# Turned sums in both chains, three PSUM rounds for the backward products, loads on another queue and split stores in a memory-transformer kernel

## The chip, the cores and the metric

The kernel runs on one core of one Trainium2 chip. The metric is device time in microseconds (us) of one execution. Ratios to "before" are each from the fast runs of the same rounds and with a 95% interval; a ratio is not quite the quotient of the medians quoted beside it. Chips differ by some tenths of a per cent (the kernel before had medians from 3278 to 3294 us), so ratios, not microseconds, are compared across batches. One per cent is 33 us.

## The reference, cut to what matters

The function is a transformer block whose attention runs segment by segment with a memory of 8 rows handed from each segment to the next. The kernel computes the output and all gradients.

```python
for s in range(n_seg):                       # 2048 rows, 64 segments of 32 rows
    h = concat([mem, xs])                    # 8 memory rows + 32 rows
    q, k, v = h@Wq, h@Wk, h@Wv               # 32 heads of 128
    p = softmax(mask(q k^T * scale))
    o = (p v) @ Wo                           # back to 512 columns
    mem = o[:, :8]; outs.append(o[:, 8:])
y = x + attention(layernorm(x)) + squared_relu_mlp(layernorm(x))
# returned: y and the gradients of x, mem0, Wq, Wk, Wv, Wo, w1, b1, w2, b2
```

Memory makes 64 forward steps and 64 backward steps strictly serial. These are the *forward chain* and the *backward chain* below. Work on the 8 memory rows that can wait is done per block of four steps; its instructions are called *leftover* here, and their names begin with `L.`

## The kernel before

The four engines read one ordered list of short operation names. Each engine executes its own operations in the order of that list and waits on semaphores where data is missing. A name's last digit is the half of the heads (0 or 1).

A backward step goes as follows. The gradient of the step's output, GT, is projected (`o0mm o1mm`), copied to SBUF as gON (`o0ev o1ev`), turned (`o0fl o1fl`) and copied as gOT (`o0te o1te`). Products of short vectors give the gradient of v (`vp`). Scores (`s0 s1`) and four VectorE instructions (`d1 d2 d3 d4`) give the softmax gradient gS; the last of them, `d4`, writes gS. `tu` turns gS. Products with gS give the gradients of k and q (`kp`, `qp`). Each product round lands in PSUM and is copied out ("evicted") to gv, gk, gq, with `e` for the 32 rows of the step and `l` for the 8 rows of memory. Six *gathers* (`vg kg qg`, 16 matmuls each) sum everything into one PSUM bank, R. R holds four row groups of 32 which must be added up and turned to give the next step's GT.

Before, the adding was a copy, a matmul against a selection matrix, a copy, and a transpose:

```python
def sm():                                    # 4 matmuls: adds the row groups
    ps["n"] = alloc("ps_sum")
    for c in range(DC):
        nc.tensor.matmul(ps["n"][SEG * c:SEG * c + SEG, 0:P], lhsT=sel[:], rhs=R4()[:, c * P:(c + 1) * P],
                         start=True, stop=True, tile_position=(0, SEG * c), skip_group_check=True)
def sF():
    ps["F"] = F()
    ENGS[pre + "sF"](ps["F"][:], ps["n"][:, 0:P])
def sT():
    nc.tensor.transpose(ps["n"][:, P:2 * P], ps["F"][:], identF[:])
    ...
```

Products used six rounds a step (v0 v1 k0 q0 k1 q1), all in the same pair of PSUM tiles, with 20 evictions. The list for one of the four steps of a block, the loads and the stores:

```python
B_ORDER = (
    "o0mm o0ev xt- L.xt- o1mm o0fl vp0 L.lq o1ev o0te o1fl s0 vea0 veb0 o1te ldq- ldn- L.qo ldk- vtr vg0 "
    "vlb0 d10 vla0 vp1 d20 d30 s1 L.G0 veb1 L.H0 d11 vlb1 vla1 d40 vea1 d21 tu0 kp0 kea0 klb0 keb0 d31 vg1 "
    "d41 kla0 qp0 qea0 qeb0 ldp kg0 tu1 kp1 kea1 klb1 L.sx- keb1 kla1 qg0 qp1 ldn qea1 qeb1 L.ra0 kg1 qg1 "
    "ra L.G1 sm vc sF L.H1 sT HT",
    ...                                      # three more steps, cut
# ---- cut ----
o["ldq"] = lambda: dma(tile_of("qN", [P, GW])[:], rows[:, GW:2 * GW])      # dma = nc.sync.dma_start
...
def vc():                                    # assembles vT for the next step's scores
    vT = tile_of("vT", [P, KH, HG, L])
    nc.gpsimd.tensor_copy(vT[:, :, :, 0:SEG], C["vl"][:])
    nc.gpsimd.tensor_copy(vT[:, :, :, SEG:L], B_["vTL"][:, :, :, lc])
```

## Time and profile before

The time before is 3290.86 us (two runs, 3289.17 to 3292.55). Of the profiled execution these are the head of the page, with the busy time of engines (and their share of the span and instruction count), the TensorE clock in 40 slices (9 is full), and the DMA queues (packets, MB, share of the 16 DMA engines).

```profile
span 3266.8 us, 115469 instructions
PE 2704.2 (83%) x51673; PEld 1338.9 (41%) x51768; DVE 1220.4 (37%) x3526; ACT 1017.1 (31%) x2492; POOL 193.7 (6%) x345
PEclk9999899999999999966799999999999988999999
q1 hardware_dynamic: 890418, 625.81, 77.0%
q8 instruction: 406, 6.65, 0.8%
```

PE is the line that everything hangs on. Its idle time is the loss. So the view to read is PE's waits, taken for the backward chain alone (from its first projection to its last, 1602 to 2608 us). Columns: the waiting instruction, what it waited for, then total us, number of waits, longest.

```profile
PE b_pp L563 <- issue: 45.8, 34, 4.7
PE ps_gR L478 <- issue: 18.5, 15, 2.8
PE ps_proj L437 <- DVE GT L424: 17.9, 63, 0.3
PE ps_sum L497 <- ACT F L421: 17.3, 47, 0.4
PE ps_sum L489 <- ACT R L421: 13.3, 18, 0.8
PE b_pp L563 <- DMA b_qN<-S_A: 12.3, 11, 2.7
PE ps_sc L458 <- DVE gOT L424: 3.5, 16, 0.2
PE b_pp L563 <- DVE gS L522: 1.8, 4, 0.7
```

The largest item is "issue", time in which PE waited for nothing the profile shows. All lines of that kind sum to 73.8 us. The trace shows next to these gaps a 16 KB instruction page that starts late: the 2.94 us gap at 1860.01 us has its page start 0.47 us into it. I call them *page stalls*.

| stage | us |
|---|---|
| forward chain, first to last projection | 890.6 |
| backward chain, first to last projection | 1005.4 |
| from there to the end (weight gradients) | 659 |

### The profile page before, as it was taken

What the parts mean: (1) busy time and instruction counts of PE and PEld (TensorE: products, weight loads), DVE (VectorE), ACT (ScalarE), POOL (GpSimd) and SP (SyncE); (2) the same over time, 40 slices, a digit from 0 to 9 for tenths busy, and PEclk for the clock granted to TensorE, in tenths of its full rate; (3) what the DMA queues carried; (4) which work ended last, traced back from release to release, by engine and by line L of the source; (5) the groups of instructions that cost most, each with busy time, mean ns of one, the idle gap of its engine ahead of it and who ended that gap; (6) DMA issues with size and microseconds to landing.
All of it is one profiled execution on the core that took longest, in us unless ns stands there. A gap on an engine that the chain in (4) does not pass through costs nothing.

```text
span 3266.8 us, 115469 instructions
## 1 busy us (share of the span) xinstructions
PE 2704.2 (83%) x51673; PEld 1338.9 (41%) x51768; DVE 1220.4 (37%) x3526; ACT 1017.1 (31%) x2492; POOL 193.7 (6%) x345
## 2 busy tenths in 40 slices
PE   8898778888888888834688888888888866999998
PEld 4453334444444444412344344344344423444444
DVE  4440035555655555523344344444444400010001
ACT  3331124444444444412333333333333401111111
POOL 0000000000000000000000010010000000000000
PEclk9999899999999999966799999999999988999999
DMA  9958894676667676689668666666776699999993
GB/s 254 283 145 312 293 291 114 165 179 162 185 164 184 161 184 161 171 235 256 185 164 210 166 164 181 189 164 172 190 183 172 173 260 199 205 186 224 187 187 91
DMA packets 890915, 633.20 MB, mean 194 GB/s; under 512 B 659745, under 2 KB 748466, under 8 KB 881074
## 3 DMA queue, kind: packets, MB, share of 16 engines
q1 hardware_dynamic: 890418, 625.81, 77.0%
q8 instruction: 406, 6.65, 0.8%
q14 instruction: 91, 0.75, 0.1%
HBM read 227.16 MB, written 250.10 MB: 146 GB/s over the span
## 4 chain that ended last, share of the span: by engine, by line
PE 57%; DMA 13%; SPq 13%; DVE 7%; issue 5%; ACT 5%; ACTq 0%; POOLq 0%; POOL 0%; DVEq 0%
PE ps_gR L478 11%; PE ps_proj L437 11%; PE ps_gw L1364 8%; SPq L1289 6%; PE b_pp L563 3%; PE ps_R L478 3%; DMA S_GOL<-l_gON 3%; PE ps_tr L167 2%; ACT R L421 2%; PE ps_sum L489 2%; PE ps_L L406 2%; DMA out_dram<-wt 2%; PE ps_w L366 2%; PE ps_w L386 1%; PE ps_RL L1071 1%
## 5 line engine op out<-in xcount | busy, mean ns | idle before, releaser
L1364 PE MATMUL ps_gw<-gn,HNc 128*128 128x512 bf16 x1881 | 416.5, 380 | 8.3 <-ACT wt L1339 6.3
L437 PE MATMUL ps_proj<-Wqkv,X 128*32 128x512 bf16 x6144 | 361.9, 385 | 18.2 <-DVE X L424 17.9
L1364 PEld LDWEIGHTS <-HNc 128*128 128x128 bf16 x1920 | 188.2, 98 | 231.9 <-issue 9.5
L421 ACT CAST f_N<-ps_proj 128x512 bf16<-128x512 f32 x320 | 185.4, 583 | 258.0 <-PE ps_proj L437 243.7
L1339 ACT CAST wt<-ps_gw 128x512 bf16<-128x512 f32 x126 | 69.5, 591 | 541.8 <-DMA out_dram<-wt 353.1
L437 PEld LDWEIGHTS <-X 128*32 128x32 bf16 x6144 | 156.9, 98 | 174.7 <-DVE X L424 29.9
L1322 DVE TENSOR_TENSOR gx<-ps_rows,gb 128x512 f32<-128x512 f32 x16 | 11.1, 692 | 427.5 <-PE ps_rows L1320 396.8
L1364 PE MATMUL ps_gw<-GOc,gn 128*128 128x512 bf16 x627 | 142.2, 387 | 19.2 <-DMA gn<-S_ON 18.3
L478 PE MATMUL ps_gR<-WT,b_gq 128*32 128x512 bf16 x2048 | 145.2, 401 | 7.8 <-issue 7.5
L478 PE MATMUL ps_gR<-WT,b_gk 128*32 128x512 bf16 x2048 | 145.8, 404 | 5.8 <-issue 5.7
L478 PE MATMUL ps_gR<-WT,b_gv 128*32 128x512 bf16 x2048 | 142.5, 393 | 7.6 <-issue 7.5
L437 PE MATMUL ps_proj<-WoT,GT 128*32 128x512 bf16 x2048 | 125.6, 388 | 22.5 <-DVE GT L424 17.9
L478 PE MATMUL ps_R<-Wo,OT 128*32 128x512 bf16 x2048 | 127.1, 390 | 0.0
L1145 POOL COPY b_vT<-b_vl 128x1024 bf16<-128x1024 bf16 x64 | 66.7, 1042 | 905.9 <-PE ps_sc L458 521.4
L421 ACT CAST gON<-ps_proj 128x512 bf16<-128x512 f32 x128 | 75.0, 586 | 118.9 <-PE ps_proj L437 115.2
L489 PE MATMUL ps_sum<-R,sel 128*32 128x128 f32 x1152 | 61.2, 285 | 58.4 <-ACT R L421 53.0
L1364 PEld LDWEIGHTS <-gn 128*128 128x128 bf16 x640 | 63.6, 100 | 96.4 <-DMA gn<-S_ON 18.6
L406 PE MATMUL ps_L<-Wqkv,XL 128*128 128x512 bf16 x376 | 84.8, 385 | 18.2 <-DMA XL<-S_XL 16.8
L421 ACT CAST b_gq<-b_pp 128x256 bf16<-128x256 f32 x128 | 47.7, 373 | 161.4 <-PE b_pp L563 153.3
L421 ACT CAST b_gk<-b_pp 128x256 bf16<-128x256 f32 x128 | 47.8, 373 | 150.7 <-PE b_pp L563 115.5
L424 DVE CAST b_gq<-b_pp 128x256 bf16<-128x256 f32 x128 | 54.4, 425 | 107.0 <-PE b_pp L563 102.8
L437 PEld LDWEIGHTS <-GT 128*32 128x32 bf16 x2048 | 49.5, 98 | 78.4 <-DVE GT L424 30.0
(214 smaller groups left out, 4427.9 us busy)
## 6 DMA issues: line engine op xcount, KB each, us to landing
S_A<-f_N SPq DMA_DIRECT2D x64, 512.0 KB
out_dram<-wt SPq DMA_DIRECT2D x154, 128.0 KB
S_A<-f_N SPq DMA_DIRECT2D x64, 256.0 KB
S_ON<-OC SPq DMA_DIRECT2D x64, 256.0 KB
b_qN<-S_A SPq DMA_DIRECT2D x64, 256.0 KB
b_kN<-S_A SPq DMA_DIRECT2D x64, 256.0 KB
S_GB<-b_gv SPq DMA_DIRECT2D x16, 1024.0 KB
S_GB<-b_gk SPq DMA_DIRECT2D x16, 1024.0 KB
```

What stands on the lines that cost most here:

```text
L167: nc.tensor.transpose(ps_ap, in_ap, ident[base:base + k, base:base + k])
L366: nc.tensor.matmul(ps[:], lhsT=aN[:, rc, fc * P:(fc + 1) * P], rhs=gN[:, rc, :], start=(rc == 0), stop=(rc == TC - 1))
L406: nc.tensor.matmul(ps[:], lhsT=XL[:, dc, q * P:(q + 1) * P], rhs=Wqkv[:, dc, c0:c0 + 512], start=(dc == 0), stop=(dc == DC - 1))
L421: nc.scalar.copy(out, in_)
L437: nc.tensor.matmul(ps[32 * g:32 * g + 32, :], lhsT=hT[:, dc, :], rhs=W[:, dc, c:c + 4 * P], start=(dc == 0), stop=(dc == DC - 1), tile_pos ...
L478: nc.tensor.matmul(R[32 * g:32 * g + 32, :], lhsT=XT(k, g), rhs=W[:, g * KH + k, :], start=(first and k == 4 * h), stop=(last and k == 4 * ...
L489: nc.tensor.matmul(ps["n"][SEG * c:SEG * c + SEG, 0:P], lhsT=sel[:], rhs=R4()[:, c * P:(c + 1) * P], start=True, stop=True, tile_position= ...
L563: nc.tensor.matmul(o, lhsT=N_[32 * g:32 * g + m, kk * P:(kk + 1) * P], rhs=X(kk)[32 * g:32 * g + m], start=(i == 0), stop=(i == len(jobs) ...
L1145: nc.gpsimd.tensor_copy(vT[:, :, :, 0:SEG], C["vl"][:])
L1289: nc.sync.dma_start_transpose(t_[:, b, :].rearrange("p (k e) -> p k e", k=KH), blocks(b)[:, g].rearrange("p k r -> p (k r)"))
L1339: nc.any.tensor_copy(wt[:], ps[:])
L1364: nc.tensor.matmul(ps[:], lhsT=l(rc), rhs=r(rc), start=(n == 0), stop=(n == RC_ALL - 1))
```

## The change

Intent: shorten the serial tail of each step (three PSUM crossings become two), save instructions and PSUM rounds in the backward products, take loads off the SyncE queue where they stand behind stores, and halve the 1 MB stores. The core of the diff, with cuts:

```diff
-    def sum_ops(o, alloc, R4, F, st, pre=""):        # sm sF sT: select matmul, copy, transpose
+    def turn_ops(o, alloc, R4, st):                  # ta tb: four float32 transposes of R
+            nc.tensor.transpose(st["T"][:, c * P:(c + 1) * P], R4()[:, c * P:(c + 1) * P], identF[:])
+    def over_groups(out, T, rows):                   # then one reduction over the row groups
+            nc.vector.tensor_reduce(out, T[:].rearrange("p (c g r) -> p c r g", c=DC, g=HG)[:, :, rows], ...)
...
-            def ra():                                # one copy of R
+            def ra(h):                               # two half copies: ra on ScalarE, rb on VectorE
...
-                    outer(pp("k", p), p, ...)        # six rounds: v0 v1 k0 q0 k1 q1
+                    outer(pp(p), p, ...)             # three: v (both halves), k0+q0, k1+q1
+                    outer(pp(p), p, ..., 4 * KW)     # q beside k, at a column offset
...
-            o["ldq"] = lambda: dma(tile_of("qN", ...
+            o["ldq"] = lambda: pdma(tile_of("qN", ...  # pdma = nc.gpsimd.dma_start; 320 loads in all
...
-                o[n + "o"] = lambda n=n, t=t: dma(S_GB[b, t], B_["g" + n][:]...)
+                for x in range(2): ...               # two half stores of 512 KB
...
 B_ORDER = (
+        "L.xt- o0mm vtr xt- o1mm L.lq o0ev o0fl o1ev o0te vp0 vp1 o1fl L.sx- vea veb o1te s0 s1 L.G0 vc d10 d20 "
+        "vla vlb d30 d40 vg0 d11 tu0 d21 kp0 qp0 kea0 keb0 kla0 klb0 qea0 qeb0 d31 d41 ldp vg1 L.H0 tu1 kp1 ldq "
+        "qp1 ldn ldk kg0 L.ra0 kea1 keb1 qea1 qeb1 kla1 klb1 qg0 kg1 qg1 L.G1 ra rb L.H1 ta tb HT",
```

ScalarE has `o1te vea vla vlb` among others, VectorE the `d` instructions, `veb keb0 klb0 qeb0`.

## The prediction

> **What bounds the kernel.** The page gives PE 2704 of 3267 us busy (83%); DVE 37%, ACT 31%. By stretches of the timeline: forward chain 486-1390 us (64 steps, 14.1 us each), backward chain 1600-2640 (64 steps, 16.2 us each); the change touches only these. In both, PE is the line and its idle time is the loss (waits of PE). Forward: 78 us around the sums of a step (on R 39, on F 21, on X 18), 38 on OT and ET. Backward (1640-2630): 76 us "issue" in 56 stalls of up to 4.7 us, mostly after the 1 MB block stores, so I read them as late instruction pages behind long packets; 47 us around the sums; 12 us on qN, 2 on kLs.
>
> **The sums.** Chain of waits: from the last gather matmul to the next projection 2.18 us (ACT copy 0.59, select matmul 0.47, copy 0.28, transpose 0.34, cast 0.20, rest hops). After: two 128x256 copies (ACT 0.37, DVE 0.42), four float32 transposes (four took 0.66), one reduction of 128 elements (the strided 128x32<-128x128 reduction took 0.37). Both copies read one PSUM bank. The trace has ACT's XT copy waiting for DVE's GT cast of the same bank (15 times, 9.7 us), and the Trainium skill, "PSUM — Partial Sum Buffer", on bank collisions, says two engines must not touch one bank at once, so I expect rb behind ra: 0.37+0.42+0.44+0.37 plus hops, 1.85 us. Gain 0.3 us a step, 20 us per chain; were the copies parallel, 0.7 us. XT becomes a strided reduction on DVE (0.6 instead of 0.25 us), off the path; the leftover's four reductions (1.2 us on DVE, before 0.27 on ACT) hold the first forward step of each block some 0.5 us: 8 us back. Forward: -12 us.
>
> **Backward rounds.** Rounds did not stall PE before (b_pp waits on no eviction). Four ACT/DVE instructions a step go, which were not on the path. The new order makes PE wait: walking one step with traced durations, o1te stands behind the 0.59 us eviction vea on ACT, so the second score group waits about 0.6 us; d31 and d41 stand behind keb0, klb0, qeb0 on DVE, so kp1 waits about 0.7 us with only part filled by leftover gathers. Clean step about 15.0 instead of 14.4 us, tail gain included: +40 us.
>
> **Queues.** Loads on GpSimd no longer queue behind waits on SP (SP's waits: 203 us for gS, 143 for b_pp): the 14 us on qN and kLs go. The Trainium skill, "DMA: Bandwidth & Descriptors", on issuing engines, says all queues share 16 DMA engines, so bytes cost the same; this trace has no GpSimd DMA. Half-size stores should shorten the instruction stalls; I take off 45 of 76 us, the least certain term.
>
> **Sum.** 3291 - 12 + 40 - 14 - 45 = about 3260 us. Range 3200 to 3325. Chances: faster by over 2% 0.26, within 2% 0.66, slower 0.08.
>
> **Right or wrong.** Right if: rb starts when ra ends; PE idle on X/GT near 0.4 us a step; new PE waits on gOT (ACT) and on gS near 0.6 us a step; no waits on qN; "issue" waits of PE under 40 us; forward chain shorter by 10-20 us, backward by 0-40. Wrong if: the copies run in parallel (50 us faster); stalls of issue vanish (30 faster) or stay or grow with a third ring (45 slower); GpSimd's descriptor work delays b_vT or the loads; the new waits are filled.

## The result, and the profile after

The time after is 3337.03 us (two runs, 3333.58 to 3340.49). The ratio is 1.0144, with a 95% interval of 1.0119 to 1.0168: slower, by less than 2%, and 77 us from the 3260 predicted, outside its range. The same head of the page for the kernel after:

```profile
span 3331.8 us, 113823 instructions
PE 2735.0 (82%) x50873; PEld 1372.5 (41%) x50968; DVE 1373.4 (41%) x3701; ACT 921.3 (28%) x2124; POOL 370.6 (11%) x665
PEclk9999889999999999766898998999899987999999
q1 hardware_dynamic: 876658, 556.06, 69.0%
q0 software_dynamic: 22528, 69.75, 7.1%
```

PE has 800 fewer instructions and yet 31 us more busy time. The clock row shows one reason: more 8s in the second half. GpSimd's busy time includes its DMA issues. PE's waits in the backward chain after (1586 to 2663 us):

```profile
PE ps_sc L456 <- ACT gOT L419: 41.7, 61, 0.7
PE b_pp L563 <- DVE gS L522: 39.8, 53, 0.9
PE b_pp L563 <- issue: 36.6, 22, 3.4
PE ps_proj L435 <- DVE GT L498: 24.2, 63, 0.4
PE ps_gR L476 <- issue: 19.0, 18, 4.1
PE ps_sum L485 <- ACT R L419: 10.1, 18, 1.0
PE b_pp L563 <- DMA b_qN<-S_A: 5.7, 1, 5.7
PE b_pp L563 <- DMA b_P<-S_A: 5.3, 2, 4.9
```

Two waits that were 5.3 us are now 81.5, one of each nearly every step. Page stalls went from 73.8 to 65.4 us. The forward chain went from 890.6 to 868.2 us, the backward chain from 1005.4 to 1076.4, the rest to the end from 659 to 669.

How the two waits arise can be read from the timeline of one step after (start us, duration us, engine, line, operation; in brackets the idle time before it and what ended it):

```profile
2142.99 0.59 ACT L419 CAST gv<-b_pp 128x512 bf16<-128x512 f32 x1 [0.52 <-PE b_pp L563]
2143.15 0.28 PE L456 MATMUL ps_sc<-b_vT,gOT 128*32 128x40 bf16 x16
2143.48 0.59 ACT L419 COPY gOT<-ps_tr 128x512 bf16<-128x512 bf16 x1
...
2144.12 0.28 PE L456 MATMUL ps_sc<-b_vT,gOT 128*32 128x40 bf16 x16 [0.69 <-ACT gOT L419]
...
2144.56 1.04 POOL L1144 COPY b_vT<-b_vl 128x1024 bf16<-128x1024 bf16 x1 [10.74 <-PE ps_sc L456]
2144.71 1.07 DVE L522 SCALAR_TENSOR_TENSOR gS<-ds_t,b_P 128x160 bf16<-128x160 f32 x1
```

The gOT copy (`o1te`) stands behind the eviction of gv (`vea`) on ScalarE, so the second scores wait 0.69 us. The instruction that writes gS took 1.07 us while GpSimd copied vT; its usual time is 0.33 us. The Trainium skill, "SBUF — State Buffer", section "Who interferes with whom", says that a VectorE instruction with two SBUF inputs contends with a GpSimd instruction that reads SBUF. This trace agrees: 57 of 126 gS instructions took over 500 ns, against 9 before, where the vT copy mostly fell elsewhere, and each of the 57 ended 0.17 to 0.19 us after the vT copy that it had begun in. Yet this slow instruction, in all 57 cases that of the first half, is not what PE mostly waits for. Of the 39.8 us of waits on gS 37.0 stand before the second k product, which needs the second half's `d41`, and `d41` stands behind three VectorE evictions (`keb0 klb0 qeb0`) in the list.

The half copies of R did not overlap. The group of the VectorE half (count, busy us and mean ns, then idle time before it and what ended it):

```profile
L422 DVE COPY R<-ps_gR 128x256 f32<-128x256 f32 x64 | 27.2, 425 | 245.1 <-ACT R L419 245.1
```

All its wait is for the ScalarE half. The Trainium skill, "PSUM — Partial Sum Buffer", section "PSUM bank collisions raise a hardware error", gives as the simple form of its rule that accesses to one bank are to be guarded by semaphores; the program orders the two copies, as this line shows.

**Accounting by three terms.** In the next section each run's backward chain is split into PE idle time, time lost to the half clock, and the rest. The trace has clock records of 3.413 us or a multiple at half speed; PE busy time inside them, halved, is the time lost. These sums are worked out from the trace, one profile for each kernel, so some 10 us of either may be chance. The profiled run of the kernel before was a quick one (3268.5 us, 22 us under its median of two), so the two profiles differ by more (65 us) than the medians do (46 us).

| backward chain | length | PE idle | lost to half clock | rest of PE busy |
|---|---|---|---|---|
| before | 1005.4 | 156.7 | 34.3 | 814.4 |
| after | 1076.4 | 207.2 | 56.5 | 812.8 |

So of 71 us, 50 are idle and 22 the clock. The chain has 385 fewer matmul records (24847 before, 24462 after). They come from the turned sums, as k1 below, with six rounds, has 24462 too; what they save is within the noise of the last column.

### The profile page after: what moved, and what is told of

Read it like the earlier page. It is cut to its first block, busy times and chain, and to the rows that moved or that the text cites. A ratio compares the mean times of both kernels' runs of the same rounds, so it can differ in the third digit from the quotient of the medians.

```text
span 3331.8 us, 113823 instructions
## 1 busy us (share of the span) xinstructions
PE 2735.0 (82%) x50873; PEld 1372.5 (41%) x50968; DVE 1373.4 (41%) x3701; ACT 921.3 (28%) x2124; POOL 370.6 (11%) x665
## 3 DMA queue, kind: packets, MB, share of 16 engines
q0 software_dynamic: 22528, 69.75, 7.1%
## 4 chain that ended last, share of the span: by engine, by line
PE 57%; DVE 12%; DMA 11%; SPq 10%; issue 5%; ACT 5%; POOL 0%; ACTq 0%; POOLq 0%; DVEq 0%
PE ps_gw L1367 11%; PE ps_proj L435 11%; PE ps_gR L476 9%; SPq L1292 4%; PE ps_R L476 3%; PE b_pp L563 3%; PE ps_sum L485 3%; DMA S_GOL<-l_gON 3%; PE ps_RL L1071 2%; PE ps_L L404 2%; PE ps_tr L165 2%; DVE gS L522 2%; PE ps_w L364 1%; PE ps_w L384 1%; ACT gON L419 1%
## 5 line engine op out<-in xcount | busy, mean ns | idle before, releaser
L476 PE MATMUL ps_gR<-WT,gk 128*32 128x512 bf16 x2048 | 160.0, 431 | 11.7 <-issue 11.7
L476 PE MATMUL ps_gR<-WT,gq 128*32 128x512 bf16 x2048 | 156.3, 421 | 6.4 <-issue 6.3
L435 PE MATMUL ps_proj<-WoT,GT 128*32 128x512 bf16 x2048 | 123.9, 384 | 28.2 <-DVE GT L498 24.2
L485 PE MATMUL ps_sum<-identF,R 128*128 128x128 f32 x576 | 118.0, 298 | 32.8 <-ACT R L419 29.9
L476 PE MATMUL ps_gR<-WT,gv 128*32 128x512 bf16 x2048 | 141.4, 394 | 1.5 <-issue 1.4
L419 ACT CAST gk<-b_pp 128x256 bf16<-128x256 f32 x128 | 47.7, 373 | 304.4 <-PE b_pp L563 303.8
L422 DVE COPY R<-ps_gR 128x256 f32<-128x256 f32 x64 | 27.2, 425 | 245.1 <-ACT R L419 245.1
L808 POOL COPY kM<-f_kT 128x256 bf16<-128x256 bf16 x64 | 25.8, 402 | 807.0 <-ACT f_kT L419 623.6
L485 PEld LDWEIGHTS ps_sum<-identF,R 128*128 128x128 f32 x576 | 58.8, 141 | 113.5 <-ACT R L419 70.8
L1367 PEld LDWEIGHTS <-gn 128*128 128x128 bf16 x640 | 63.7, 100 | 101.5 <-DMA gn<-S_ON 23.5
L422 DVE CAST gk<-b_pp 128x256 bf16<-128x256 f32 x128 | 54.4, 425 | 121.0 <-PE b_pp L563 121.0
```

Of the source, the lines that this page charges most:

```text
L419: nc.scalar.copy(out, in_)
L422: nc.vector.tensor_copy(out, in_)
L435: nc.tensor.matmul(ps[32 * g:32 * g + 32, :], lhsT=hT[:, dc, :], rhs=W[:, dc, c:c + 4 * P], start=(dc == 0), stop=(dc == DC - 1), tile_pos ...
L476: nc.tensor.matmul(R[32 * g:32 * g + 32, :], lhsT=XT(k, g), rhs=W[:, g * KH + k, :], start=(first and k == 4 * h), stop=(last and k == 4 * ...
L485: nc.tensor.transpose(st["T"][:, c * P:(c + 1) * P], R4()[:, c * P:(c + 1) * P], identF[:])
L1367: nc.tensor.matmul(ps[:], lhsT=l(rc), rhs=r(rc), start=(n == 0), stop=(n == RC_ALL - 1))
```

## The experiments

Theories at the start. **Order**: the loss is the order of operations around the three rounds (the two new waits). **Queue** (rival): it is the GpSimd queue. **Stores** (rival): the split stores. Beside these, the turned sums should be a gain by themselves. I ran fifteen kernels, all correct, in four batches.

| run | what it is | median us | ratio | 95% interval |
|---|---|---|---|---|
| k1 | before + turned sums | 3260.0 | 0.9939 | 0.9915-0.9964 |
| k2 | before + three rounds with the new order | 3339.1 | 1.0179 | 1.0141-1.0217 |
| k3 | after, loads on SyncE | 3290.8 | 1.0026 | 0.9993-1.0059 |
| k4 | after, whole stores | 3338.2 | 1.0183 | 1.0155-1.0212 |
| m1 | k3, gOT copy before the v evictions | 3292.4 | 1.0032 | 1.0007-1.0056 |
| m2 | k3, vT copied on ScalarE | 3261.3 | 0.9942 | 0.9904-0.9979 |
| m3 | m1 + m2 + gS chain before evictions | 3274.8 | 0.9979 | 0.9962-0.9995 |
| m4 | m3, loads on GpSimd | 3311.5 | 1.0089 | 1.0058-1.0119 |
| m5 | k1, loads on GpSimd | 3288.5 | 1.0000 | 0.9963-1.0037 |
| n1 | m2, first gk gather before second k product | 3234.0 | 0.9829 | 0.9802-0.9857 |
| n2 | n1, leftover product between the scores | 3228.3 | 0.9811 | 0.9784-0.9837 |
| n3 | m2, 64 block loads on GpSimd | 3274.2 | 0.9955 | 0.9922-0.9987 |
| p1 | after, first gk gather before second k product | 3303.2 | 1.0023 | 0.9986-1.0059 |
| p2 | n2, loads on GpSimd | 3264.5 | 0.9916 | 0.9877-0.9954 |
| p3 | n2, vT copied on GpSimd | 3242.9 | 0.9842 | 0.9812-0.9872 |

### The four parts, one at a time

**k1_sums_only.** The kernel before with `turn_ops`, `over_groups` and the half copies of R; six rounds, SyncE loads and whole stores stay.

> The kernel before with the turned sums in both chains and nothing else of the change. First theory (the backward loss is the new order of the three rounds): this part is a gain, forward chain 936.8 to about 915 us, backward 63 tails shorter by a few tenths of a us each, so 3255 to 3272 us, ratio 0.989 to 0.994. If the split copy of the reduction onto two engines and the longer reductions on the VectorE are what costs in the backward chain, it is 3290 us or more and the backward chain from its first to its last projection is over 1015 us (1005 before).

The time came out as expected, a gain of 0.6% or 20 us, but not where I said: the forward chain gives it (874.2 us, 16 less than before; the 936.8 of the expectation runs on to the first projection of the next stage), and the backward chain (1009.3 us) does not become shorter. In that chain PE idle time fell by 12 us only, because 17.3 us of waits on F went while the wait on GT rose from 17.9 to 24.2 us and loads of qN were waited for 11 us more. The half clock took as much (34.3 to 45.9 us).

**k2_rounds_only.** The kernel before with the three rounds and the new order:

```diff
-    vp -> round v0, round v1;  kp, qp -> rounds k0 q0 k1 q1;  old B_ORDER
+    round v; round k0+q0; round k1+q1;  B_ORDER of after, with "sm sF sT" for "rb ta tb"
```

> The kernel before with the three rounds and the new order of the backward chain, old sums, loads on the SyncE queue, stores whole. First theory: the loss is here, the backward chain is about 1075 to 1095 us (1005 before, 1076 after), the waits of the PE on the copy of gOT and on gS are together 60 us or more (5 before, 81 after), half-clock time in the chain over 100 us, total 3350 to 3375 us, ratio 1.018 to 1.026. Rival (the GpSimd queue, or the stores, cost the time): the rounds alone stay within 15 us of before, 3276 to 3306 us.

The waits of the Order theory came out: 44.0 us on gOT, 41.1 on gS. The chain (1057.6 us), the time (3339.1 us) and the ratio (1.0179) all lie a little under the ranges I gave. The rounds in this order, on top of the old sums, cost 59 us.

**k3_sp_loads.** One line of after: `pdma = nc.sync.dma_start`.

> The kernel after with its loads back on the SyncE queue. First theory: within 12 us of after, ratio to before 1.010 to 1.018, the same waits on gOT and gS (70 to 90 us together). Rival (the GpSimd queue is the cause): 3300 us or less, ratio below 1.004.

Here my theory missed and the rival was right: the ratio fell to 1.0026. PE's waits in its backward chain (1587.5 to 2628 us) show the two order waits unchanged:

```profile
PE ps_sc L456 <- ACT gOT L419: 42.7, 61, 0.8
PE b_pp L563 <- DVE gS L522: 38.8, 51, 0.8
PE b_pp L563 <- issue: 34.5, 24, 3.5
PE ps_gR L476 <- issue: 11.1, 14, 1.7
```

So the loads on the GpSimd queue cost another 0.0118 (against after, other chip) to 0.0157 (against k4, same chip, but k4 has whole stores too) of 3290 us, 39 to 52 us, and both causes are real.

The parts do not simply add: k1 and k2 together would make 1.0118, and k3, which has both and the split stores, is at 1.0026. Part of this can be read from the waits: PE waited 27.9 us for the copy F in k2 (17.3 before), which the turned sums remove, and the 23.5 us on qN in k1 are gone in k3. The rest is not explained.

**k4_whole_stores.** After with three whole stores for a block instead of six halves.

> The kernel after with the block stores whole again (three of them for a block instead of six). First theory: within 8 us of after, ratio to before 1.012 to 1.017. Rival (the split stores, with more DMA issues that stall on late instruction pages): 3320 us or less, ratio below 1.009.

It is no faster than after. Its page stalls are 69.2 us, against 65.4. Theory Stores falls: with the loads on GpSimd, halving the stores neither cost nor gained anything that shows. With the loads on SyncE no run changes the stores alone; the page stalls are 46.1 us in k2 (whole stores) and 56.0 in k3 (split), so nothing there points to shorter stalls either.

### What the waits are worth

**m1_o1te.** k3 with the gOT copy ahead of the v evictions:

```diff
-    vp0 vp1 o1fl ... vea veb o1te s0 s1
+    vp0 o1fl o1te vp1 ... vea veb s0 s1
```

> The kernel after with loads on the SyncE queue (ratio to before 1.0026), and in the backward order only one thing moved: the flip of the second half of gON and its copy to gOT now stand before the second v product and so before the evictions of the v round on the ScalarE. Theory of the order: the PE's wait of the scores on the ScalarE copy of gOT (42.7 us there) falls under 8 us, the backward chain from 1040 to 1000-1015 us, ratio 0.989 to 0.997. Rival (the time is bound elsewhere, a mended wait comes back as another): ratio stays 0.999 or more and another wait grows by 25 us or more.

The wait went, and the time did not follow. PE's waits in m1's backward chain (1585 to 2628.5 us):

```profile
PE b_pp L563 <- DVE gS L522: 36.5, 51, 0.8
PE b_pp L563 <- issue: 35.2, 28, 3.4
PE ps_gR L476 <- issue: 21.5, 20, 2.5
PE ps_sc L456 <- ACT gOT L419: 13.1, 58, 0.2
```

The next table tells where it was given back. It has the median time from a step's start to the start of a group of matmuls, worked out from the trace (62 steps of each).

| group | k3 | m1 | m2 | n1 |
|---|---|---|---|---|
| second scores (s1) | 4.22 | 3.73 | 4.22 | 4.22 |
| first k product (kp0) | 6.03 | 5.61 | 5.95 | 5.95 |
| second k product (kp1) | 8.64 | 8.23 | 8.42 | 8.55 |
| second q product (qp1) | 9.03 | 8.62 | 8.84 | 8.90 |
| gather gk0 | 9.42 | 9.12 | 9.27 | 7.58 |
| gather gq0 | 10.48 | 10.59 | 10.14 | 9.53 |
| transposes of the sum | 14.70 | 14.81 | 14.06 | 13.22 |

m1 did more than was meant: its gS instruction is fast too (mean 330 ns, 2 of 126 over 500 ns, against 630 ns and 52 in k3), since in the median step it now begins 5.14 us after the step's start and the long vT copy ends at 5.21. So both were mended, the wait on gOT and the slow gS, for no gain in time. Up to the last product m1 is 0.4 us ahead of k3. By the gather gq0 it is behind. Page stalls rose from 56.0 to 65.8 us in m1, and the time lost to the half clock from 45.2 to 57.3 us, both mainly in the gathers. I read this so: a wait in front of the product bursts had covered the late instruction pages, and without it PE waited for the pages instead. That is an inference from one profile of each kernel. That the freed time did not reach the end is measured.

**m2_vt_act.** k3 with vT copied by ScalarE in a slot in which it was idle:

```diff
-    nc.gpsimd.tensor_copy(vT[:, :, :, 0:SEG], C["vl"][:])           # and the 8 memory rows
+    nc.scalar.copy(vT[:, :, :, 0:SEG], C["vl"][:])
-    s0 s1 L.G0 vc d10 d20 vla vlb d30 ...
+    s0 s1 L.G0 d10 d20 vla vlb vc d30 ...
```

> The same kernel as for m1 but its order kept, only the copies of vT moved from GpSimd to ScalarE, behind the evictions of the v round. Theory that the GpSimd copy slows the VectorE's gS instruction: its mean falls from 630 ns to 330-380 ns and none is over 500 ns; the wait of the products on gS falls from 39 us to 15-28 us; ratio 0.993 to 1.000. Rival (only the place of the second half's chain behind three evictions makes that wait): gS instructions are short but the wait stays at 33 us or more and the time within 6 us of 1.0026.

The gS group in after and in m2, in that order, within their backward chains:

```profile
L522 DVE SCALAR_TENSOR_TENSOR gS<-ds_t,b_P 128x160 bf16<-128x160 f32 x126 | 83.2, 661 | 4.3
```

```profile
L522 DVE SCALAR_TENSOR_TENSOR gS<-ds_t,b_P 128x160 bf16<-128x160 f32 x126 | 41.0, 325 | 4.3
```

The instruction is twice as fast and none is over 500 ns. The time fell by 0.0084, 28 us. But the wait on gS stayed at 35.8 us, as the rival said, because what waits there is the second k product, for `d41` behind three evictions. By the table m2 is 0.2 us ahead of k3 at the second products and 0.6 us ahead at the transposes of the sum, so most of the gain came in the gathers: page stalls fell from 56.0 to 42.6 us, and the half clock took 9 us less. The 28 us are measured for moving the copy. That the fast gS gave them is not shown: in m1 gS was as fast, and nothing was gained.

**m3_all.** m1 and m2, and `d11 d21 d31 d41` directly behind `tu0`, ahead of the evictions of the first k/q round.

> Both of these and the second half's softmax-gradient chain put before the VectorE's evictions of the first k/q round; loads on SyncE. Theory of the order: the waits on gOT and gS together fall from 81 us to 25 us or less, half-clock time in the chain falls by 10 us or more, chain 965 to 1000 us, ratio 0.975 to 0.989, so faster than both kernels of the change. Rival (the three rounds are slow because evictions and products no longer overlap, whatever the order): the waits come back as waits on gk, gv or b_pp's evictions of 40 us or more, ratio 0.995 or more.

The waits on gOT and gS are 14.0 us together, and yet m3 is not faster than m2. The evictions became the wait (gq, 20.6 us), page stalls came to 66.2 us (42.6 in m2) and the half clock took 54.3 us (35.9 in m2). As a theory of the time, "take the two waits away and the loss is gone" falls with m1 and m3.

**n1_kg0_first.** m2, with useful work put where the gS wait is, instead of taking the wait away:

```diff
-    vg1 ... tu1 kp1 ldq qp1 ldn ldk kg0 kea1 ...
+    vg1 ... tu1 kg0 kp1 ldq qp1 ldn ldk kea1 ...
```

> m2 (vT copied on ScalarE, loads on SyncE, ratio 0.9942), with one thing changed in the TensorE's order: the gather of the first half of gk stands before the second k product instead of behind the second q product, so that it fills the wait for gS. Theory of the order: the wait of the products on gS falls from 36.7 us under 8 us and comes back in the time, 20 to 40 us, ratio 0.982 to 0.988. Rival (the PE's late instruction pages and the half clock take back what a mended wait frees): the wait falls, stalls marked as issue rise by 12 us or more, or the half-clock time by 20 us or more, ratio 0.990 to 0.998.

One moved name gave 0.0113, 37 us. The first gather of gk needs only the first round's evictions, so it could run in the 0.75 us in which PE waited for gS. PE's two largest waits in m2 (1588 to 2601 us) were:

```profile
PE ps_sc L456 <- ACT gOT L419: 42.4, 61, 0.7
PE b_pp L563 <- DVE gS L522: 35.8, 47, 0.9
```

In n1 (1594 to 2571 us) no wait on gS is left in the list:

```profile
PE ps_sc L456 <- ACT gOT L419: 42.8, 61, 0.7
PE b_pp L563 <- issue: 27.9, 28, 2.9
PE ps_gR L476 <- issue: 17.2, 18, 2.6
```

Page stalls rose by 10 us (42.6 to 52.3), less than expected by the rival, and the half clock took 8 us less.

**n2_fill_both.** n1 with a leftover product between the two scores in three of four steps:

```diff
-    s0 s1 L.G0
+    s0 L.G0 s1
```

> n1, and in three of four steps a leftover product of the block put between the scores of the first and the second half, so that it fills the wait for gOT as well. Theory of the order: the wait on gOT falls from 43 us to 10-15 us, time another 10 to 25 us under n1, ratio 0.974 to 0.984. Rival: within 8 us of n1, as with m1, in which the same wait was taken away for no gain.

The wait on gOT fell to 11.8 us. The gain over n1 is 0.0018, 6 us, with intervals that overlap. As in m1, this wait gave next to nothing, though here it was filled with useful work: page stalls rose from 52.3 to 68.4 us.

```profile
PE b_pp L563 <- issue: 38.0, 41, 3.0
PE ps_gR L476 <- issue: 21.2, 23, 2.5
PE ps_sc L456 <- ACT gOT L419: 11.8, 18, 0.7
```

n2 beats both kernels of the change: 1.9% under before, 3.3% under after (0.9811 over 1.0144). It keeps the turned sums, the three rounds and the split stores.

### The GpSimd queue

**m4_all_gps.** m3 with the loads on the GpSimd queue, whose engine now does little else.

> m3 with the loads on the GpSimd queue as in the change, whose engine now does nothing but issue them. If the queue itself costs (late first loads, late instruction pages, lower clock): 25 to 50 us over m3, chain 20 us or more longer. If it cost only because the vT copies shared the engine: within 12 us of m3.

It is 0.0110 slower, 36 us, so sharing the engine with the vT copies is not the reason. The gS instruction stays at 325 ns with none over 500 ns. That says nothing of whether issuing DMAs would slow it, because none of the 126 coincided with one of GpSimd's DMA issues.

**m5_sums_gps.** k1 (six rounds) with the loads on the GpSimd queue.

> The kernel before with the turned sums (ratio to before 0.9939) and its loads moved to the GpSimd queue, no three rounds. If the queue costs by itself: the last DMA issue to the end of the span takes about 9.4 us instead of 2.7, the first step of the backward chain 4 us or more longer, and more stalls of the PE, so ratio 1.001 to 1.008 (25 to 45 us over the sums alone). If it cost only together with the three rounds: ratio 0.997 or less, 10 us or less over the sums alone.

It is 0.0061 slower, 20 us, a little under the range I gave but far over the rival's. Page stalls in its backward chain are 102.0 us, against 70.7 in k1.

**n3_block_gps.** m2 with only the 64 block loads on the GpSimd queue.

> m2 with only the four loads of a block (64 of 320 issues) on the GpSimd queue. If the queue has a fixed cost: from the last DMA issue to the end of the span 9.4 us instead of 2.7, and little else, 5 to 16 us over m2, ratio 0.9955 to 0.999. If every load on it costs alike, 64 of 320 of some 35 us and the fixed part: 11 to 16 us; if any use of it slows the whole chain, 25 us or more, ratio 1.002 or more.

It is 0.0013 over m2, within the noise; the profile is clearer than the time. The last DMA issue of the program, in k3 and in after (the spans end at 3287.4 and 3331.8 us):

```profile
3284.66 0.33 SPq L1338 DMA_DIRECT2D out_dram<-gi  x1
```

```profile
3322.40 0.33 SPq L1338 DMA_DIRECT2D out_dram<-gi  x1
```

From its end to the end of the span k3 takes 2.4 us and after 9.1 us. Every kernel with all loads on the GpSimd queue (after, k4, m4, m5, p1, p2) has 15.1 us from PE's last matmul to the end of the span, every one without (before, k1 to k3, m1 to m3, n1, n2, p3) has 8.4 us, and n3, with 64 of the 320, has 11.7 us. The trace shows the place: GpSimd's last DRAIN, an instruction that closes the program on each engine, takes 9.84 us in the six, 6.50 us in n3 and 1.24 to 1.25 us in the others. So 6.7 us of the queue's cost is at the very end, after all work, and grows with the use of the queue.

**p1_after_kg0.** After itself with only `kg0` moved, as in n1.

> The kernel after itself (GpSimd loads, GpSimd copies of vT), with only the first gather of gk moved in front of the second k product. If the order of the three rounds makes a cost of its own there as well: the wait on gS falls from 40 us under 12 us, time 25 to 45 us under after, ratio 1.001 to 1.008. If with the GpSimd queue the stalls on late pages take it back: ratio 1.011 or more, with the stalls marked as issue 20 us or more over after's 65.

The ratio is 1.0023 against after's 1.0144: one moved name makes up for the loss to within the interval, 40 us. The wait on gS went from 39.8 to 2.0 us. Page stalls rose to 87.6 us, so part of the time was taken back, but not most of it.

**p2_fill_gps.** n2 with the loads on the GpSimd queue.

> n2 (ratio 0.9811) with the loads on the GpSimd queue. If the queue's cost adds to whatever order stands: 20 to 45 us over n2, ratio 0.987 to 0.995, stalls marked as issue in the chain 10 us or more over n2's 68, last DMA issue to the end of the span 6 to 7 us longer. If the cost came from the waits of the old order: within 10 us of n2.

The cost is 0.0105, 34 us, with the waits of the old order gone. So it is the queue's own. PE's waits in p2 (1586 to 2589.5 us), to be held against n2's above:

```profile
PE b_pp L563 <- issue: 42.0, 35, 3.3
PE ps_gR L476 <- issue: 25.8, 23, 2.9
PE ps_sc L456 <- ACT gOT L419: 12.4, 18, 0.7
```

The pairs side by side (page stalls and half clock of the backward chain in us). The kernels of a pair differ in nothing but the loads; only m3 and m4 ran on one chip, so the others are compared by their ratios to before:

| pair, loads on SyncE / GpSimd | ratio | page stalls | lost to half clock | last matmul to end |
|---|---|---|---|---|
| k1 / m5 | +0.0061 | 70.7 / 102.0 | 45.9 / 32.6 | 8.4 / 15.1 |
| k3 / after | +0.0118 | 56.0 / 65.4 | 45.2 / 56.5 | 8.4 / 15.1 |
| m3 / m4 | +0.0110 | 66.2 / 84.5 | 54.3 / 57.3 | 8.4 / 15.1 |
| n2 / p2 | +0.0105 | 68.4 / 82.3 | 35.6 / 44.5 | 8.4 / 15.1 |

Page stalls rise in each pair, by 9 to 31 us. The smaller rises alone could be chance, as the kernels with loads on SyncE range from 42.6 to 73.8 us, but all four point the same way. The page transfers themselves do not become longer (mean 1.02 us in k3, 1.02 in after; 1.02 in k1, 1.00 in m5), nor the time from a page's start to the end of the gap (median 2.43 us in k1, 2.40 in m5), so PE's pages must start later relative to when it needs them. Why they do is not shown by any record here. Nor are page stalls the whole of it: in the first new-rounds pair (k3 / after) the backward chain grew by 36 us, of which 9 are page stalls, 12 waits on the loads themselves (2.7 to 14.9 us) and 11 the half clock.

**p3_fill_pool.** n2 with the vT copies back on GpSimd.

> n2 with the vT copies back on GpSimd (loads on SyncE). If the slow gS instruction still costs once the waits are filled: gS mean 600 ns or more, 15 to 30 us over n2, ratio 0.986 to 0.990. If it only mattered because the products waited on gS: within 8 us of n2, ratio 0.979 to 0.9835.

The difference is 0.0031, 10 us, between the two expectations, with overlapping intervals. gS is at 601 ns again and a wait on gS of 20.4 us is back, all of it at the first k product: the leftover product that stood before it now fills the wait for gOT instead. But the 10 us do not lie in the backward chain, which is 979.8 us in p3's profile and 984.4 in n2's; they lie in the rest to the end, where no gS is computed (668.0 against 656.8). So no cost of the slow gS is shown here.

## Why the prediction was wrong

**Right.** Both new waits were named with cause and size: 0.6 and 0.7 us a step, 82 us together for 63 steps; the trace has 81.5. `rb` starts when `ra` ends, as said. The forward chain gave 22.4 us (12 predicted, 10 to 20 in its list; too small, but on the right side). The wait on GT stayed at 0.4 us a step. But the size of a wait was not its worth: filling the wait on gS gave 37 us (n1) and 40 us (p1), while the wait on gOT gave next to nothing, removed (m1) or filled (n2).

**Roughly right.** "Clean step ... +40 us". With loads on SyncE, the rounds and split stores on top of the turned sums cost 0.0087 (k3 over k1), 29 us, page stalls included. The prediction carried the sums' gain in this term, so the split between terms can only be compared roughly. It did not see that the vT copy would move next to the gS instruction and slow it (0.33 to 1.07 us); what that cost is not shown (m1, m2 and p3 disagree).

**Wrong: the paragraph "Queues".** This is the step that failed. It said that on the GpSimd queue "the 14 us on qN and kLs go", and that half-size stores "should shorten the instruction stalls; I take off 45 of 76 us". Together that is 59 us of gain. Measured: the loads on the GpSimd queue cost 34 to 39 us on the new rounds and 20 on the old, in four pairs that differ in nothing else (52 against k4, which differs in the stores too). The split stores gave nothing that shows with the loads on GpSimd (k4). The page stalls after are 65.4, not under 40 us. The waits on qN and kLs, 14.2 us before, are 9.0 after, but P and kN add 5.9 (2.3 before), so hardly any of the 14 us came. Between a gain of 59 and a loss of 39 (after against k3) there are 98 us, more than the whole miss of 77; the other terms came out some 20 us better than predicted (28 us of loss predicted, 9 measured in k3).

The prediction leaned on the Trainium skill, "DMA: Bandwidth & Descriptors", section "Issuing engines are not separate DMA queues", for bytes costing the same on any queue. The trace agrees within about a tenth: the 69.75 MB took 7.1% of the span of all 16 DMA engines on the new queue, 237 us, and the old queue's time fell by 216 us. The step from "the bytes cost the same" to "the queue costs nothing" was mine. The prediction's own list had "stay or grow with a third ring (45 slower)" among what would make it wrong; that line came true and deserved a far higher weight, since no trace of this kernel had a GpSimd DMA.

**What stays open.** Why instruction pages come later with the software queue, and why GpSimd's last DRAIN takes longer after it, is not explained. The half-clock term varies by 10 us between profiles of near kernels, and I have one profile for each, so its share in any single pair is uncertain. That page stalls take back freed time rests on three cases (m1, m3, n2) of one profile each, and on their times, which agree.

## What to carry to other kernels

The length of a wait is not what its removal is worth. Here the wait on gOT gave next to nothing, whether it was removed (m1) or filled with a leftover product (n2); the wait on gS gave nothing when it was removed at the cost of later evictions (m3) and its whole length when a ready gather filled it (n1, p1). In m1, m3 and n2 page stalls grew as the waits went. So test each wait by itself: walk one step on every engine, ask which ready instruction could stand in the wait, and time it; here one moved name was worth 37 us. Treat a queue that the trace does not yet have as a cost to be measured alone, and watch what an off-path engine's copy will newly overlap with.

## What the Trainium skill lacked or had wrong

- "DMA: Bandwidth & Descriptors", "Issuing engines are not separate DMA queues": this section gives only the sequencer's issue time as what differs between issuing engines. The page treats the GpSimd path further in other sections, but I found no cost to instruction pages there. Moving 320 loads (69.75 MB) from SyncE to GpSimd cost 0.0061 to 0.0118 of the time in four pairs (20 to 39 us), with page stalls of TensorE up by 9 to 31 us.
- No page that I found says that a program with GpSimd DMAs ends later: from the last matmul to the end of the span 8.4 us without them, 11.7 us with 64, 15.1 us with 320 (GpSimd's last DRAIN 1.24, 6.50 and 9.84 us).
- "Runtime: NRT & Kernel Launch", "Instruction fetch mechanics": it calls the cost of crossing a 16 KiB block "mostly hidden". Here PE stalled for pages 56 times, 73.8 us in 1005 us, in the chain before, and between 42.6 and 102.0 us in the other kernels' backward chains.
- "TensorE: Matmul & The Clock Gate", "Why this matters for your kernels": it advises against PE-idle gaps over about 3 us (another section of the page has drops under frequent short idles, without a figure). In the chain after, clock records went from full to half 25 times, and in the 3.413 us ahead of each the longest idle gap was 1.65 us on average and as short as 0.69 us; PE was idle for 60% of those stretches on average, 26% at least. The record length of 3.413 us agrees with the page.
- "SBUF — State Buffer", "Who interferes with whom": nothing wrong; confirmed for a GpSimd copy (1.07 against 0.33 us).
